# Linear attention ahead of two expert layers: a result tile per unit of work, keys requested first, identity transposes while they arrive, routing in portions, projection ahead of the turning

## The chip, the cores and the metric

One Trainium2 chip, one of its cores. The metric is the device time of one launch in microseconds (us). All times below are from one profiled execution of the kernel before, or from its timed runs.

## The reference

The inputs are q, k and v of shape 4 x 8 x 576 x 64 (batch, heads, positions, head width) and w_phi, 64 x 128. Only the first stage matters here in detail:

```python
def phi(x):
    proj = np.einsum('bhsd,df->bhsf', x, w_phi)
    proj = proj - np.max(np.abs(proj), axis=-1, keepdims=True)
    return np.concatenate([np.exp(proj), np.exp(-proj)], axis=-1)
q_p, k_p = (phi(q), phi(k))
kv = np.einsum('bhsf,bhsd->bhfd', k_p, v)
z = np.sum(k_p, axis=2)
num = np.einsum('bhsf,bhfd->bhsd', q_p, kv)
den = np.einsum('bhsf,bhf->bhs', q_p, z)[..., None] + 1e-06
return (num / den).astype(np.float32)
```

Its result, as x of 2304 rows by 512, goes through a first expert layer: rows with `x @ w_skip > 0` choose one of 8 experts by `argmax(x @ w_gate)`, go through `relu(x @ w1[e]) @ w2[e]`, are scaled by the softmax value and added to x. A second layer runs all rows through all 8 experts of a second set of weights and sums them with a normalized weight per row and expert.

## The kernel before

The kernel runs three stages: attention (to about 262 us), the first expert layer (to about 430 us) and the second.

**Attention** (function `attention`). The 4 batches are taken in two pairs (`bp`), the 8 heads in four pairs (`hp`), which gives 8 units. A unit has 9 blocks j of 128 rows (two batches x 64 rows), so there are 72 block numbers w. Work goes through 36 steps g and one more. Each step takes two pairs of blocks, as a rule one of keys and one of queries (only keys in the first three steps). For TensorE (PE in the profile) a step is: turn the next step's blocks (`transp`, tile `pt`, copied by ScalarE to `th`), project this step's blocks with w_phi (`proj`, tile `pp`), and then, for the step before: turn the features of its queries (`q_tr`, `ptq`, copied to `fq`), fold w_gate and w_skip into a finished key-value product (`augment`, tile `pa`, some steps only), add its keys to that product (`kv_mm`, `kv`), and multiply queries by it (`num`, `po`). VectorE (DVE) subtracts the row maximum of the projection (`center`: `m`, then `t`), ScalarE (ACT) makes the two exponentials (`expo`: `f`). `finish` on DVE divides `po` into the tile `x` and into the routing scores `lall`. `pp` has one buffer in PSUM; `pt`, `ptq`, `pa`, `po` and the routing's `pr` share four in turn (tag W).

**The tile x** holds a whole pair of batches, 128 x 9 x 512, and has one buffer. After a unit's last block its 128 columns are stored to DRAM by SyncE's queue (SP): three copies for the first pair (xd0, xd, x2d), two for the second.

**Routing of the first pair** starts when its last unit is finished, in step 21: `lg` is summed from `lall` and `Router.route` runs in one piece on DVE, 15 instructions from `mx` to `ohb`. `stepped`, called at each step's end, takes one entry of `gates`: nothing, then `route2` (ranks by small matmuls `pr`, then `rk` to `di`), then the store of `gate` into column 512 of xd0 and xd, 4 bytes per row. Nine scatters of row numbers follow on GpSimd (POOL). In step 25 `early(g)` advances `moe1`: `early_slots` picks the two fullest slots in one piece of 26 small DVE instructions, `fetch` requests their row list, rows and weights (w1 to `r1`), `fetch2` w2. In steps 28 to 35 one eighth of w1 is split per step (`split_w1`: `w1h` on ACT, `w1l` on DVE).

**What sets the order.** In the loop over the steps PE, DVE and ACT keep the order of the code (`manual_schedule`). SP and POOL are ordered by a scheduler. Each engine and each queue works in order. At the start `aug`, the table for `augment`, is cleared and filled by DVE and two small DMAs, and the routing's constants are made by POOL with type changes on DVE.

Of the kernel before, what the change touches and what calls it, by code (L numbers as in the profile page):

```python
# [38 lines left out]
def attention(tc, nc, cp, q, k, v, w_phi, w_gate, w_skip, lgs, routed, stepped, early, last_steps):  # L39
# [3 lines left out]
    with ExitStack() as ctx:  # L43
# [13 lines left out]
        nc.sync.dma_start(aug[0:64, :, 65:73], w_gate.rearrange("(h d) e -> d h e", d=DH))  # L57
        nc.sync.dma_start(aug[0:64, :, 73:74], w_skip.rearrange("(h d o) -> d h o", d=DH, o=1))
        for h in range(H):
            nc.vector.tensor_copy(aug[:, h, 0:65], ident[0:65, 0:65])  # L60
# [10 lines left out]
        def load(nm, u):  # L71
# [12 lines left out]
            for b in range(2):  # L84
                pr = slice(64 * b, 64 * b + 64)
                s = {"qt": q, "kt": k, "vt": v}[nm][2 * bp + b, 2 * hp : 2 * hp + 2]
                if nm == "vt":
                    for h in range(2):
                        nc.sync.dma_start(
                            t[:, 5 * b : 5 * b + 4, h, 0:DH], s[h, 0:512].rearrange("(p j) d -> p j d", j=4)  # L90
                        )
                    nc.sync.dma_start(t[pr, 4, :, 0:DH], s[:, 512:576].rearrange("h p d -> p h d"))
                elif nm == "kt":
                    nc.sync.dma_start(
                        t[:, :, 5 * b : 5 * b + 4], s[:, 0:512].rearrange("h (p j) d -> p h j d", j=4)
                    )
                    nc.sync.dma_start(t[pr, :, 4], s[:, 512:576].rearrange("h p d -> p h d"))
                else:
                    (nc.sync if u else nc.scalar).dma_start(t[pr], s.rearrange("h (p j) d -> p h j d", j=NJ))
# [116 lines left out]
        def finish(ws_, po):  # L216
# [5 lines left out]
            for i, m in ((0, n),) if one else [(i, 1) for i in range(n)]:  # L222
                u, j = divmod(ws_[i], NJ)
                bp, hp = units[u]
                if ("x", bp) not in st:
                    st["x", bp] = c1.tile([P, NJ, D], F32, name="x", tag="x", bufs=1)
                x = st["x", bp]
                nc.vector.tensor_tensor(
                    x[:, j : j + m, hp * P : hp * P + P].rearrange("p j (h d) -> p h j d", h=2),
# [31 lines left out]
        late, aug_todo, t, f, prev, fin = [], [], None, None, [], []  # L261
# [35 lines left out]
def constants(tc, nc, keep, pool):  # L297
# [5 lines left out]
    for nm, op in (("upper", ALU.is_gt), ("ones", None)):  # L303
        t = (pool if op else keep).tile([P, P], F32, name=nm + "_f")
        nc.gpsimd.memset(t, 1.0)
        if op is not None:
            nc.gpsimd.affine_select(
                out=t, in_=t, compare_op=op, fill=0.0, base=0, pattern=[[1, P]], channel_multiplier=-1
            )
        b = pool.tile([P, P], BF16, name=nm)  # L310
        nc.vector.tensor_copy(b, t)
        c[nm] = b
        c[nm + "_f"] = t

    def iota(nm, pattern, shape, base=0):
# [3 lines left out]
        nc.vector.tensor_copy(f, i)  # L319
# [23 lines left out]
class Router:  # L343
# [9 lines left out]
    def route(self, bp, lg):  # L353
# [10 lines left out]
        sm = self.tile([NJ, 1], "sm")  # L364
        v.tensor_reduce(sm, ex, AX.X, ALU.add)
        v.tensor_scalar(sm, sm, 1e-9, None, ALU.add)
        v.reciprocal(sm, sm)
        gate = self.tile([NJ, 1], f"gate{bp}")
        v.tensor_tensor(gate, sm, do, ALU.mult)

# [3 lines left out]
        v.scalar_tensor_tensor(oh, oh, -float(E), c["iej"], ALU.mult, ALU.add)  # L374
        am = self.tile([1, NJ], "am")
# [5 lines left out]
        self.half = bp, gate, do, ohb  # L381
        return gate

    def route2(self):
        nc, c, v = self.nc, self.c, self.nc.vector
        bp, gate, do, ohb = self.half
# [49 lines left out]
    def early_slots(self):  # L436
# [4 lines left out]
        r = []  # L441
        for i in range(2):
# [23 lines left out]
            r.append(ti)  # L466
# [8 lines left out]
        return r  # L475
# [48 lines left out]
def moe1(tc, nc, c, rt, w1, w2, idx, xd, xd0, x2d, route, end):  # L524

    with ExitStack() as ctx:
# [10 lines left out]
        def fetch(s):  # L537
            t, i = (first[s], 0) if s < 2 else (tabs[1], s - 2)
            e = nc.sync.value_load(t[0:1, 0, i : i + 1], min_val=0, max_val=E - 1)
            r = nc.sync.value_load(t[0:1, 1, i : i + 1], min_val=0, max_val=NIDX - SLOT)  # L540
            src, n = (xd0, NTOK // 2) if s < 2 else (xd, NTOK)
# [11 lines left out]
            for a in range(2):  # L553
# [7 lines left out]
                )  # L561
            for kb in range(NKB):
# [3 lines left out]
            return e  # L566
# [107 lines left out]
        first = rt.early_slots()  # L674
        fetch2(fetch(0))
        done, psA = 0, None
# [458 lines left out]
def tile_kernel(  # L1135
# [32 lines left out]
    def early(g):  # L1168
        if g == 25 or 28 <= g < 36:
            next(m1)  # L1170

    def route(bp, psum):
        rt.psum = psum
        gate = rt.route(bp, lgs[bp])

        def go():
            for t in dsts(bp)[:-1]:
                nc.sync.dma_start(t[:, :, D : D + 1], gate)

        if bp == 0:  # L1180

            gates.extend([lambda: None, rt.route2, go])
        else:
            rt.route2()
# [55 lines left out]
```

## Time and profile before

| | us |
|---|---|
| timed runs | 2041.30, 2045.28, 2044.95 (median 2044.95) |
| profiled execution | 2041.64 |
| its span, first to last instruction | 2039.9 |
| PE busy in the span | 1979.4 (97%) |
| DVE, ACT, POOL busy | 1258.9, 898.1, 336.5 |

The span is nearly the whole of the profiled execution: 1.7 us lie outside it. The profiled execution is at the lower end of the runs, 3.3 us below their median. A row of a timeline gives the start in us, the duration, the engine (PEld is PE's weight load, a q behind the name the engine's queue), the line, the operation, output and inputs with their shapes, how many were merged, and in brackets how long the engine was idle before and what ended that. PE's float32 matmuls show as two records each, so x16 is 8 matmuls of the code.

### The profile page before, as it was taken

The numbers are of one execution on the slowest core, as the hardware profiler recorded it, in microseconds if no ns is written. First come the engines' busy times: TensorE is split into PE (matmuls) and PEld (weight loads), VectorE is DVE, ScalarE is ACT, GpSimd is POOL, SyncE is SP. The second block draws the span as 40 slices with busy tenths as digits, with TensorE's granted clock in tenths as the row PEclk, the third lists the DMA queues.
The fourth block names the chain that finished last, engine by engine and source line by source line (L and its number), as shares of the span: only waits on it lengthen the run. The fifth ranks groups of instructions, "written<-read, shape, count | busy, mean of one in ns | idle before, by whom it ended". The sixth has DMA issues, their size and how long they took to land.

```text
span 2039.9 us, 30601 instructions
## 1 busy us (share of the span) xinstructions
PE 1979.4 (97%) x11711; PEld 1743.2 (85%) x11711; DVE 1258.9 (62%) x2150; ACT 898.1 (44%) x1705; POOL 336.5 (16%) x271
## 2 busy tenths in 40 slices
PE   7996999998999999999999999999999999999999
PEld 5775788996789999998888989989888999999897
DVE  4454677676576666666655666666665566666663
ACT  4663755454544344334343443433434344334341
POOL 1002032221111211211112112121201211212210
PEclk9998999999999999999999999999999999999999
DMA  6784767654321221212122122122212221211211
GB/s 155 105 122 66 166 143 271 229 190 152 119 73 42 83 73 52 83 64 92 47 68 83 51 74 78 47 83 71 84 47 68 83 73 52 83 61 64 83 52 42
DMA packets 163354, 187.39 MB, mean 92 GB/s; under 512 B 38334, under 2 KB 116926, under 8 KB 163196
## 3 DMA queue, kind: packets, MB, share of 16 engines
q1 hardware_dynamic: 159292, 177.58, 31.0%
q0 software_dynamic: 3456, 7.09, 1.0%
q8 instruction: 94, 1.54, 0.3%
q10 hardware_dynamic: 448, 0.66, 0.1%
q14 instruction: 64, 0.52, 0.1%
HBM read 163.70 MB, written 23.96 MB: 92 GB/s over the span
## 4 chain that ended last, share of the span: by engine, by line
PE 70%; DMA 3%; DVE 2%; ACT 1%; SPq 0%; issue 0%; ACTq 0%
PE py L991 36%; PE pb L955 14%; PE pd L955 9%; PE pa L955 9%; DMA r<-in_moe_w_dram 3%; PE pg L832 1%; PE warm L705 1%; DVE wcl L782 0%; SPq L752 0%; DMA xr<-x2d 0%; ACT w2h L941 0%; PE pt L824 0%; DVE hl L976 0%; ACT xch L888 0%; DVE c L1043 0%
## 5 line engine op out<-in xcount | busy, mean ns | idle before, releaser
L991 PE MATMUL py<-w2l,hh 128*128 128x512 f32 x1152 | 451.6, 392 | 0.0
L991 PE MATMUL py<-w2h,hh 128*128 128x512 f32 x1152 | 451.3, 392 | 0.1
L991 PE MATMUL py<-w2h,hl 128*128 128x512 f32 x1152 | 450.3, 391 | 0.0
L946 DVE TENSOR_TENSOR w2l<-r,w2h 128x512 fp32r<-128x512 f32 x184 | 177.2, 969 | 207.1 <-ACT w2h L941 207.0
L991 PEld LDWEIGHTS py<-w2l,hh 128*128 128x128 f32 x1152 | 216.1, 188 | 49.0 <-issue 0.6
L991 PEld LDWEIGHTS py<-w2h,hl 128*128 128x128 f32 x1152 | 216.3, 188 | 37.4
L991 PEld LDWEIGHTS py<-w2h,hh 128*128 128x128 f32 x1152 | 216.3, 188 | 36.4 <-ACT hh L971 0.5
L1002 DVE SCALAR_TENSOR_TENSOR acc<-py,lg,acc 128x512 f32<-128x512 f32 x264 | 197.0, 746 | 68.0 <-PE py L991 67.2
L971 ACT ACTIVATE hh<-c 128x384 fp32r<-128x384 f32 x192 | 100.9, 525 | 213.3 <-DVE c L1031 118.3
L941 ACT ACTIVATE w2h<-r 128x512 fp32r<-128x512 f32 x184 | 114.7, 625 | 175.6 <-DMA r<-in_moe_w_dram 175.1
L784 POOL TENSOR_TENSOR r<-r,s 128x512 f32<-128x512 f32 x45 | 58.2, 1293 | 659.6 <-DVE wcl L782 648.3
L955 PE MATMUL pb<-xch,wch 128*128 128x384 f32 x576 | 149.2, 340 | 11.6 <-ACT v L963 9.1
L782 DVE TENSOR_TENSOR wcl<-r,wch 128x512 fp32r<-128x512 f32 x230 | 154.3, 687 | 7.2 <-ACT wch L776 6.1
L764 POOL TENSOR_TENSOR s<-r 128x512 f32<-128x512 f32 x45 | 58.0, 1288 | 586.4 <-DMA r<-in_moe_w_dram 586.4
L955 PE MATMUL pb<-xcl,wch 128*128 128x384 f32 x576 | 147.6, 337 | 0.0
L955 PE MATMUL pb<-xch,wcl 128*128 128x384 f32 x576 | 147.1, 336 | 0.0
L776 ACT ACTIVATE wch<-r 128x512 fp32r<-128x512 f32 x230 | 138.5, 622 | 10.1 <-PE pd L955 3.0
L955 PEld LDWEIGHTS pb<-xch,wch 128*128 128x128 f32 x576 | 105.2, 188 | 31.7 <-ACT v L963 13.8
L1015 DVE TENSOR_TENSOR pb<-pb,s 128x384 f32<-128x384 f32 x96 | 54.4, 566 | 122.0 <-PE pb L955 64.6
L963 ACT ACTIVATE s<-pa 128x384 f32<-128x384 f32 x96 | 47.2, 492 | 174.7 <-PE pa L955 174.7
L976 DVE SCALAR_TENSOR_TENSOR hl<-c,hh 128x384 fp32r<-128x384 f32 x192 | 106.7, 556 | 6.9 <-ACT hh L971 6.9
L963 ACT ACTIVATE z<-pb 128x384 f32<-128x384 f32 x96 | 47.1, 490 | 139.6 <-PE pb L955 139.6
(230 smaller groups left out, 3618.3 us busy)
## 6 DMA issues: line engine op xcount, KB each, us to landing
r<-in_moe_w_dram SPq DMA_DIRECT2D x168, 512.0 KB
r<-in_moe_w_dram SPq DMA_DIRECT2D x184, 256.0 KB
xd<-x SPq DMA_DIRECT2D x12, 576.0 KB
x2d<-x SPq DMA_DIRECT2D x8, 576.0 KB
xr<-x2d SPq DMA_DIRECT2D x18, 256.0 KB
out_dram<-acc SPq DMA_DIRECT2D x18, 256.0 KB
kt<-in_k_dram SPq DMA_DIRECT2D x16, 256.0 KB
vt<-in_v_dram SPq DMA_DIRECT2D x32, 128.0 KB
```

What stands on the lines that cost most here:

```text
L764: g.tensor_tensor(s1, a21, a22, ALU.add)
L776: nc.scalar.activation(wc[m, i][0], wsrc[m][i], AF.Copy)
L782: nc.vector.tensor_tensor(l, src[i], f32(h), ALU.subtract)
L784: (nc.gpsimd if m else nc.vector).tensor_tensor(src[3], src[2], src[6], ALU.subtract)
L941: nc.scalar.activation(h, w2r[m, b], AF.Copy)
L946: nc.vector.tensor_tensor(l, w2r.pop((m, b)), f32(h), ALU.subtract)
L955: nc.tensor.matmul(dst, w[:, kb, sl], x[:, kb], start=(start and m == 0), stop=(stop and m == 5), skip_group_check=True,)
L963: nc.scalar.activation(t, src, AF.Copy)
L971: nc.scalar.activation(hh, src, AF.Relu)
L976: nc.vector.scalar_tensor_tensor(hl, src, 0.0, f32(hh), ALU.max, ALU.subtract)
L991: nc.tensor.matmul(py, ht[:, i * P : i * P + P], wt, start=(m == 0), stop=(m == 11))
L1002: nc.vector.scalar_tensor_tensor(accs[t], py, lg[:, t, e : e + 1], accs[t], ALU.mult, ALU.add)
```

## The change

- `aug` is built by POOL in `load_aug`, called after the first loads; its DMAs move behind the first queries.
- Requests at the start: keys of unit 0, values of unit 0, keys of unit 1, queries of unit 0, then `aug`, then the rest. The first queries go through SP, no longer through ACT's queue.
- A tile `tab` of zeros goes through Exp as ACT's first instruction, and eight type changes of constants move from DVE to POOL.
- PE gets 41 transposes of the identity into a tile `warm` that nothing reads: 9 first, 8 behind the first turning, 16 behind the first projection, 8 in step 1.
- From step 1 on a step projects first and turns the next blocks second.
- `x` becomes 128 x 9 x 128, one tile for each unit, with three buffers.
- `route` and `route2` become one generator with two `yield`s: `mx` to the second `oh`, then `am` to `gate`, then the ranks, each a step apart. In the code the ranks now come in step 23 (before: 22) and the gate's store in 24 (before: 23); SP issues the store as soon as its queue and `gate` allow.
- `early_slots` yields after each slot. `moe1` is advanced in step 26 (first slot, with w1 requested ahead of the row list) and 27 (second slot), before in 25.

```diff
+            tab = wk.tile([P, 2, G], F32, name="tab", tag="m", bufs=4)
+            nc.vector.memset(tab, 0.0)
+            nc.scalar.activation(tab, tab, AF.Exp)
...
-        nc.vector.memset(aug, 0.0)
...
+        def load_aug():
+            nc.gpsimd.memset(aug, 0.0)
...
-                if ("x", bp) not in st:
-                    st["x", bp] = c1.tile([P, NJ, D], F32, name="x", tag="x", bufs=1)
-                x = st["x", bp]
+                if j == 0:
+                    st["x"] = c1.tile([P, NJ, P], F32, name="x", tag="x", bufs=3)
+                x = st["x"]
...
-        for nm in ("kt", "qt", "vt"):
-            load(nm, 0)
-        for nm in ("kt", "vt", "qt"):
-            load(nm, 1)
+        for nm, u in (("kt", 0), ("vt", 0), ("kt", 1), ("qt", 0)):
+            load(nm, u)
+        load_aug()
+        for nm, u in (("vt", 1), ("qt", 1)):
+            load(nm, u)
...
+            busy(9)
             th = transp(steps[0])
+            busy(8)
             for g in range(len(steps) + 1):
                 cur = steps[g] if g < len(steps) else []
-                nth = transp(steps[g + 1]) if g + 1 < len(steps) else None
                 if cur:
-                    t = center(proj(th))
-                th = nth
+                    if g:
+                        t = center(proj(th))
+                    else:
+                        nth = transp(steps[1])
+                        t = center(proj(th))
+                        th = nth
+                        busy(16)
+                    if 0 < g < len(steps) - 1:
+                        th = transp(steps[g + 1])
+                    if g == 1:
+                        busy(8)
...
-        if g == 25 or 28 <= g < 36:
+        if 26 <= g < 36:
             next(m1)
...
+            gates.extend([lambda: None, part, part, go])
...
-                go = lambda t=t: nc.sync.dma_start(t[:, :, sl], x[:, :, sl])
+                go = lambda t=t: nc.sync.dma_start(t[:, :, sl], x)
```

How the order changes. TensorE at the start, before:

```order
L108 MATMUL pt<-ident,kt 128x128 x8
L125 MATMUL pp<-ws,th 128x128 x8
L108 MATMUL pt<-ident,kt 128x128 x4
L125 MATMUL pp<-ws,th 128x128 x8
L155 MATMUL kv<-f,vt 65x256 x8
```

TensorE at the start, after (`warm` is the unread tile):

```order
L272 MATMUL warm<-ident 128x128 x9
L113 MATMUL pt<-ident,kt 128x128 x4
L272 MATMUL warm<-ident 128x128 x8
L113 MATMUL pt<-ident,kt 128x128 x4
L130 MATMUL pp<-ws,th 128x128 x8
L272 MATMUL warm<-ident 128x128 x16
L130 MATMUL pp<-ws,th 128x128 x8
L113 MATMUL pt<-ident,kt 128x128 x4
L272 MATMUL warm<-ident 128x128 x8
L160 MATMUL kv<-f,vt 65x256 x8
```

The two turnings and the projection keep their places, with transposes of the identity in front and between; the second projection now stands ahead of the third turning.

SyncE's queue at the start, before (key loads of 128x2x256 and 64x2x64, two of each per unit):

```order
DMA kt<-in_k_dram 128x2x256
DMA kt<-in_k_dram 64x2x64
DMA aug<-in_moe_w_gate_dram 64x8x8
DMA aug<-in_moe_w_skip_dram 64x8x1
DMA kt<-in_k_dram 128x2x256
DMA kt<-in_k_dram 64x2x64
```

After:

```order
DMA kt<-in_k_dram 128x2x256
DMA kt<-in_k_dram 64x2x64
DMA kt<-in_k_dram 128x2x256
DMA kt<-in_k_dram 64x2x64
DMA vt<-in_v_dram 128x4x64 x2
```

Unit 0's second half of the keys has moved ahead of the two loads of `aug`.

VectorE in step 22 (first queries of the second pair of batches, with what an instruction waits for), before:

```order
L219 TENSOR_SCALAR rd<-po 128x4 [waits PE_49]
L220 RECIPROCAL rd<-rd 128x4 [waits DVE_49]
L228 TENSOR_TENSOR x<-po,rd 128x2x2x64 [waits DMAHW4_49,DMAHW3_49,DMAHW5_49,DMAHW2_49,DMAHW6_49,DMAHW1_49,DMAHW7_49,DMAHW0_49,DVE_49]
L234 TENSOR_TENSOR lall<-po,rd 128x2x2x9
L395 TENSOR_TENSOR rk<-pr,ebase 128x72 [waits PE_49]
```

After:

```order
L224 TENSOR_SCALAR rd<-po 128x4 [waits PE_49]
L225 RECIPROCAL rd<-rd 128x4 [waits DVE_49]
L233 TENSOR_TENSOR x<-po,rd 128x2x2x64 [waits DMAHW3_49,DMAHW4_49,DMAHW2_49,DVE_49]
L239 TENSOR_TENSOR lall<-po,rd 128x2x2x9
L392 TENSOR_REDUCE am<-oh 128x9
```

The write of `x` waited for stores of the whole pair (eight DMA semaphores); now it waits for the three stores of the unit three before. What stands behind it is the second portion of the routing, no longer the ranks.

## Rows read from the trace of the kernel before

**Rows 1.** Windows: from:to, length, busy us per engine (count), TensorE clock, DMA share, GB/s.

```profile
300.00:2040.00 1740.00, 1712.91 (x8817) 1528.92 (x8815) 1089.89 (x1768) 728.05 (x1441) 303.33 (x218) 1.00 0.26 87
```

**Rows 2.** Waits of TensorE, 24 to 262 us: total, times, longest.

```profile
PE ptq L195 <- DVE rk L395: 11.1, 1, 11.1
PE po L205 <- issue: 3.7, 2, 2.6
...
PE pp L125 <- DVE rd L219: 1.8, 1, 1.8
```

**Rows 3.** Timeline of the start, 0 to 24 us.

```profile
1.21 0.28 POOL masks.py:199 TENSOR_SCALAR_AFFINE_SELECT ident<-ident 128x128 f32<-128x128 f32 x1
...
2.06 2.31 ACTq L99 DMA_DIRECT2D qt<-in_q_dram  x2
...
3.72 0.63 SPq L94 DMA_DIRECT2D kt<-in_k_dram  x1
...
9.96 1.11 PE L108 MATMUL pt<-ident,kt 128*128 128x128 f32 x4 [5.18 <-DMA vt<-in_v_dram]
...
11.01 2.08 PE L125 MATMUL pp<-ws,th 64*128 64x128 f32 x16
...
14.39 1.22 DVE L134 TENSOR_TENSOR t<-pp,m 128x1024 f32<-128x1024 f32 x1
...
17.77 5.34 PE L155 MATMUL kv<-f,vt 128*65 128x256 f32 x16
...
23.47 0.71 PE L125 MATMUL pp<-ws,th 64*128 64x128 f32 x8
```

**Rows 4.** Timeline of undisturbed steps on TensorE, 30 to 54 us.

```profile
30.80 3.62 PE L155 MATMUL kv<-f,vt 128*65 128x256 f32 x16
...
41.45 1.16 PE L125 MATMUL pp<-ws,th 64*128 64x128 f32 x16
...
47.96 1.16 PE L125 MATMUL pp<-ws,th 64*128 64x128 f32 x16
...
53.57 1.16 PE L125 MATMUL pp<-ws,th 64*128 64x128 f32 x16
```

**Rows 5.** Timeline of steps 22 to 26, all engines.

```profile
150.59 0.97 PEld L125 LDWEIGHTS pp<-ws,th 64*128 64x128 f32 x16 [0.17 <-DVE rd L220]
...
154.69 11.01 SPq L1178 DMA_DIRECT2D xd<-gate  x2
...
157.93 1.16 PE L125 MATMUL pp<-ws,th 64*128 64x128 f32 x16 [1.03 <-DVE t L134]
...
169.57 0.42 DVE L228 TENSOR_TENSOR x<-po,rd 128x256 f32<-128x256 f32 x1 [11.41 <-DMA xd<-gate]
...
177.83 1.33 PE L125 MATMUL pp<-ws,th 64*128 64x128 f32 x16
...
182.98 0.16 DVE L219 TENSOR_SCALAR rd<-po 128x4 f32<-128x4 f32 x1 [9.21 <-PE ptq L195]
...
195.14 1.16 PE L125 MATMUL pp<-ws,th 64*128 64x128 f32 x16
```

**Rows 6.** Timeline of steps 27 and 28, and the first split of w1.

```profile
202.62 1.16 PE L125 MATMUL pp<-ws,th 64*128 64x128 f32 x16 [1.79 <-DVE rd L219]
...
209.27 1.16 PE L125 MATMUL pp<-ws,th 64*128 64x128 f32 x16
...
214.97 0.61 ACT L576 ACTIVATE w1h<-r 128x512 fp32r<-128x512 f32 x1
```

**Rows 7.** Timeline of steps 11 to 13 on TensorE, 78 to 95 us.

```profile
78.11 1.16 PE L125 MATMUL pp<-ws,th 64*128 64x128 f32 x16
...
85.55 0.48 PE L205 MATMUL po<-kvf,fq 128*64 128x74 f32 x8 [2.59 <-issue]
...
86.96 2.08 PE L125 MATMUL pp<-ws,th 64*128 64x128 f32 x16
...
94.60 1.16 PE L125 MATMUL pp<-ws,th 64*128 64x128 f32 x16
```

More of the change, by code (lines that the diff above doesn't have):

```diff
@@ L259, in attention, with busy @@
                 load(nm, u)
-        late, aug_todo, t, f, prev, fin = [], [], None, None, [], []
+        late, aug_todo, t, f, prev = [], [], None, None, []
+        warm = bank([P, P], "warm")
+        def busy(n):
+            for _ in range(n):
+                nc.tensor.transpose(warm, ident, ident)
         with tc.manual_schedule(engines={nc.tensor.engine, nc.vector.engine, nc.scalar.engine}):
+            busy(9)
             th = transp(steps[0])
+            busy(8)
             for g in range(len(steps) + 1):
                 cur = steps[g] if g < len(steps) else []
-                nth = transp(steps[g + 1]) if g + 1 < len(steps) else None
                 if cur:
-                    t = center(proj(th))
-                th = nth
+                    if g:
[9 more added lines that the diff above has]
+                        busy(8)
                 tl = {m: [(2 * i + r, w + r) for i, (nm, w) in enumerate(prev) if nm == m for r in range(2)] for m in "kq"}
@@ L310, in constants @@
         b = pool.tile([P, P], BF16, name=nm)
-        nc.vector.tensor_copy(b, t)
+        nc.gpsimd.tensor_copy(b, t)
         c[nm] = b
@@ L318, in iota @@
         f = pool.tile([P] + shape, F32, name=nm)
-        nc.vector.tensor_copy(f, i)
+        nc.gpsimd.tensor_copy(f, i)
         c[nm] = f
@@ L363, in route @@
         nc.scalar.activation(ex, ex, AF.Exp)
[L364 to L369, printed above, removed]
         oh = self.tile([E, NJ], "oh")
@@ L374, in route @@
         v.scalar_tensor_tensor(oh, oh, -float(E), c["iej"], ALU.mult, ALU.add)
+        yield
         am = self.tile([1, NJ], "am")
@@ L379, in route @@
         v.tensor_tensor(ohb, oh, do.rearrange("p j o -> p o j").to_broadcast([P, E, NJ]), ALU.mult)
[L381 to L386, printed above, removed]
+        sm = self.tile([NJ, 1], "sm")
+        v.tensor_reduce(sm, ex, AX.X, ALU.add)
+        v.tensor_scalar(sm, sm, 1e-9, None, ALU.add)
+        v.reciprocal(sm, sm)
+        self.gate = self.tile([NJ, 1], f"gate{bp}")
+        v.tensor_tensor(self.gate, sm, do, ALU.mult)
+        yield
         pr = self.psum()
@@ L474, in early_slots @@
                 v.tensor_copy(self.off, eq)
-        return r
+            yield ti
     def slots(self):
@@ L540, in fetch @@
             r = nc.sync.value_load(t[0:1, 1, i : i + 1], min_val=0, max_val=NIDX - SLOT)
+            if s == 0:
+                load_r1(e)
             src, n = (xd0, NTOK // 2) if s < 2 else (xd, NTOK)
@@ L561, in fetch, with load_r1 @@
                 )
+            if s:
+                load_r1(e)
+            return e
+        def load_r1(e):
             for kb in range(NKB):
@@ L673, in moe1 @@
         rt.scatter()
-        first = rt.early_slots()
+        es = rt.early_slots()
+        first = [next(es)]
         fetch2(fetch(0))
+        yield
+        first.append(next(es))
         done, psA = 0, None
@@ L1173, in route @@
         rt.psum = psum
-        gate = rt.route(bp, lgs[bp])
+        parts = rt.route(bp, lgs[bp])
         def go():
             for t in dsts(bp)[:-1]:
-                nc.sync.dma_start(t[:, :, D : D + 1], gate)
+                nc.sync.dma_start(t[:, :, D : D + 1], rt.gate)
+        part = lambda: next(parts, None)
+        part()
         if bp == 0:
-            gates.extend([lambda: None, rt.route2, go])
+            gates.extend([lambda: None, part, part, go])
         else:
-            rt.route2()
+            part()
+            part()
             go()
```

14 lines of the change are left out of this document (5 added, 9 removed).

## The prediction

> **What bounds the kernel now.** I read the stretches first. From 300 us on TensorE is busy 1712.91 of 1740.00 us [rows 1], and the change touches nothing there but a few DVE instructions' order. So what it is worth is how much earlier the attention ends. Inside the attention I read TensorE's waits and then its step lengths, projection to projection. Undisturbed, a step with an augment takes 47.96 - 41.45 = 6.51 us and one without 53.57 - 47.96 = 5.61 [rows 4]; within such a step TensorE goes from matmul to matmul with no idle note, so TensorE is the bound and DVE and ACT have room. What exceeds 6.51 or 5.61 is loss. The losses stand in four places: the start; steps 22 to 25, with the one large wait, 11.1 us before `ptq` [rows 2]; steps 26 and 27; and a stall in step 11 [rows 7].
>
> **The change part by part.**
>
> *The start.* Before, queries go ahead on ACT's queue (2.06), the second half of unit 0's keys is requested at 3.72, and the turning that needs it starts only at 9.96, after 5.18 idle. The projection follows at 11.01, the first `kv` at 17.77 and the projection of step 2 at 23.47 [rows 3]. All of this runs at the lower clock level: the projection takes 2.08 where it takes 1.16 later, sixteen `kv` records 5.34 against 3.62 [rows 3, 4]. Now the keys stand two requests earlier and no queries compete. The identity is ready at 1.5 [rows 3]; nine transposes, a turning of four and eight more are 21 at 1.11 / 4 = 0.28, or 5.9 us, so the second turning starts at 7.4 if the keys are there. Projection at 8.3, at the higher level until 9.5; DVE needs two passes of 1.22 before `pp` is free [rows 3], so the second projection starts at 11.9. From the first projection to `kv` it was 6.76, less 0.92 for the faster projection: features are ready at 14.1. Ahead of `kv` now stand a projection (1.16), a turning (some 0.7) and eight identities (1.1), so it starts at about 14.9, runs 3.5 and lets the projection of step 2 start at 18.4. The next `kv` follows at 18.4 + 1.16 + 0.7 = 20.3, before at 23.47 + 1.16 = 24.6. Gain **4.3**. Bounds: keys landing no earlier than 9.96 leave 1.7; keys early and every identity hidden give 5.5. I take the middle of the upper part since the keys' own bytes are few once the queries are gone. The 41 identities cost nothing where PE waits anyway; uncovered, eight cost 1.1. ACT's table load and the constants go to POOL and the start, where their users come later: nothing.
>
> *x per unit.* Steps 22 to 25 take 195.14 - 150.59 = 44.55 us [rows 5]. Undisturbed they are 5.61 + 6.51 + 5.61 + 6.51 = 24.24, with some 0.6 for the ranks' small matmuls 24.8. The excess is **19.7**: 1.1 in step 22, 13.4 in step 23 (177.83 - 157.93 = 19.90 against 6.51), 5.2 in steps 24 and 25. In step 23 DVE's first write of `x` for the second pair sat 11.41 until the stores of the first pair had been read out (the row names the gate's store, issued in the same stretch; the write waits for all stores) [rows 5], and `ptq` could not have a PSUM bank because `po` and `pr` were unread. The rest of the 13.4 is the clock: after the gap matmuls ran at the lower level. Three tiles of one unit each remove this: the write in step 22 needs the stores of the unit three before, some 50 us old. Late next is nothing on DVE.
>
> The 5.2 of steps 24 and 25 I can't place. DVE's `rd` came at 182.98, 9.21 after DVE's last work, though its `po` was long done [rows 5], while POOL issued its nine scatters. If it is an effect of the gap it goes; if of the scatters or of instruction supply it stays, 0 to 5.2; I take half, 2.6. There is also a new cost. The gap was the time in which DMA drained three stores and two gate stores (SP alone issued 11.01 us on the gate [rows 5]). TensorE now works through that crowd. Rows 7 show what a crowd can do: in step 11 TensorE stopped 2.59 in the middle of `po`, waiting for nothing but issue, then ran at the lower level (2.08 for a projection); steps 11 and 12 took 16.49 against 12.12, 4.4 lost. Such waits occur twice between 24 and 262, 3.7 together [rows 2]. Bounds 0 to 4.4, taken 1.9. Left of the 19.7: **15.2** (10 to 19.7).
>
> On that stall the Trainium skill (Runtime: NRT & Kernel Launch, Instruction fetch mechanics) says that a sequencer fetches its next block of instructions while it executes the current one, and that crossing a block boundary is mostly hidden. By that the crowd costs nothing and the sum below is 1.9 better; the row with 2.59 idle speaks against it, and I go by the row.
>
> *Routing in portions.* Steps 26 and 27 take 209.27 - 195.14 = 14.13 against 11.22, 2.9 lost, 1.79 of it seen as TensorE waiting for DVE [rows 2, 6], which first did 26 small instructions of `early_slots` in one row. Halves of 11 and 15, a step apart, fit the room DVE has in a step, or nearly: gain **2.0** (1 to 2.9). The routing's own 15 instructions, halved the same way, are in the 1.1 of step 22 above.
>
> *w1 a step later, behind two stores.* Its first split starts at 214.97 with no idle [rows 6]. Requested at about 202 and behind two stores, of at most 5 us each by the drain above, the first piece lands near 214: cost 0 to 2, taken **0.5**. Behind the waiting ACT instruction would stand `th`, which TensorE's next projection needs.
>
> *Projection ahead of turning.* Same matmuls, same bound; DVE starts 0.8 earlier in each step, which only adds room. Nothing: TensorE's own row of work hides it, and if it weren't the bound the gain would be up to that 0.8 in the few steps that wait for DVE.
>
> Sum: 4.3 + 15.2 + 2.0 - 0.5 = 21.0. Against the profiled execution, 2041.64, that is 2020.6; against the median of the runs, 2044.95, it is 2024.0. The profiled execution lies at the low end of the runs, so I forecast between them: **2022**.
>
> **Rivals.** *The whole loss goes* (the 5.2 belongs to the gap, no crowd stall): 1.9 + 2.6 more, and a fetch stall like step 11's may fall elsewhere: about 2016, to 2010 if step 11's is gone too. For it: DVE's standstill began right behind the gap [rows 5]; against: scatters and DMA crowd are still there.
>
> *The gap comes back in pieces.* TensorE, DVE and ACT now run where DMA is full, and instruction stalls of 4.4 each come twice while the 5.2 stays: 21 - 2.6 - 6.9 = 11.5 left, about 2032. For it: rows 7; against: two such waits in 238 us.
>
> *No gain.* The next stage is held by something that does not move with the attention's end, a row list or weights. Then within 4 us of before, about 2043. Against it: rows 2 hold no wait of TensorE for a DMA.
>
> *Slower.* The crowd of steps 21 to 25, at 4.4 us a stall: from five stalls on (22 us) the gain is used up, six give 2047. With two such waits in all the steps between 24 and 262 [rows 2] that is very unlikely.
>
> **How the numbers follow.** A measurement here tells about 0.2% (4 us) from no change. Forecast 2022 (2017 to 2028) 0.55; whole loss goes 0.20; pieces 0.19; no gain 0.04; slower 0.02. Range: the bounds 10 + 1.7 + 1 - 2 = 10.7 and 19.7 + 5.5 + 2.9 = 28 of the terms, on either base, cut at the ends: 2011 to 2032. Faster by over 0.2%: 0.94; within: 0.04; slower: 0.02.
>
> **What would show it.** In the profile of the changed kernel the step 2 projection should start near 18.4, the write of `x` in step 22 should not wait, steps 22 to 25 should take 25 to 31 us with the clock at its higher level throughout, steps 26 and 27 near 11.5 to 12, and the first `w1h` should wait under 2. The attention should end some 21 us earlier and the span behind it be unchanged. I am wrong if the second keys still land near 10, if TensorE shows new issue waits in steps 21 to 25, or if the expert layer's first matmuls wait for a DMA.

## The result, and the profile after

The changed kernel takes 2017.68 us, the median of four runs (2020.51, 2013.0, 2017.09, 2018.27), against 2045.12 for the kernel before, timed beside it. The ratio is 0.9866, 95% interval [0.9842, 0.9890]: faster, by 1.1 to 1.6%. The forecast was 2022 with a range of 2011 to 2032. The profiled execution took 2020.51, the slowest of its four, and its span 2018.7 against 2039.9.

Where the 21.2 us of span come from is read from the starts of TensorE's projections (step g starts with projection g; before from [rows 3, 5, 6]):

| stretch | before | after | gain |
|---|---|---|---|
| start to the projection of step 2 | 23.47 | 16.81 | 6.7 |
| steps 2 to 21 | 127.12 | 122.86 | 4.3 |
| steps 22 to 25 | 44.55 | 34.39 | 10.2 |
| steps 26 and 27 | 14.13 | 11.22 | 2.9 |
| step 28 to the first expert matmul | 53.77 | 54.52 | -0.8 |
| from there to the end | 1776.86 | 1778.90 | -2.0 |

The last row is the same work: 9081 matmul records in the one trace and 9080 in the other. What remains is a change of the attention, and so a total of 23.2 us there. The split is that of one profile: a second profile of the changed kernel, taken for the last experiment, gives gains of 7.1, -0.8, 12.0, 2.9, -0.8 and -1.8 in the same rows, since its stalls were of other sizes. The first expert matmul marks its end, here in the timeline of before and then of after (start, duration, engine, line, operation):

```profile
263.04 0.74 PE L613 MATMUL ph<-xTh,w1h 128*128 128x256 f32 x4
```

```profile
239.80 0.38 PE L635 MATMUL ph<-xTh,w1h 128*128 128x256 f32 x1
```

**The start**, TensorE's timeline of after, which answers to [rows 3]:

```profile
1.54 2.18 PE L272 MATMUL warm<-ident 128*128 128x128 f32 x9 [1.54 <-POOL ident masks.py:199]
...
6.35 0.69 PE L113 MATMUL pt<-ident,kt 128*128 128x128 f32 x4
6.96 1.16 PE L130 MATMUL pp<-ws,th 64*128 64x128 f32 x16
...
10.81 1.16 PE L130 MATMUL pp<-ws,th 64*128 64x128 f32 x16 [0.79 <-DVE t L139]
...
13.26 3.62 PE L160 MATMUL kv<-f,vt 128*65 128x256 f32 x16
16.81 1.16 PE L130 MATMUL pp<-ws,th 64*128 64x128 f32 x16
```

The second turning ran at 6.35 instead of 9.96, the projection took 1.16 instead of 2.08, and step 2 was reached at 16.81 instead of 23.47. The clock column of the profile reads 1.00 in both starts, so the lower level is read from these durations; the first clock record in the trace, the higher level, begins at 21.2 us before and at 6.5 after, when TensorE had run identities and turnings since 1.54.

**TensorE's waits**, 24 to 262 us (total, times, longest), which answers to [rows 2]:

```profile
PE pa L187 <- issue: 3.7, 2, 2.3
PE ptq L200 <- issue: 1.5, 3, 0.8
...
PE po L210 <- issue: 0.4, 1, 0.4
PE pp L130 <- DVE rd L224: 0.4, 1, 0.4
```

The wait of 11.1 for `rk` is gone, and the wait for `rd` fell from 1.8 to 0.4. What is left, mostly, has no releaser but "issue": 5.6 us in these rows. The kernel before had as much, since beside the 3.7 of [rows 2] stands a row that isn't shown there:

```profile
PE ptq L195 <- issue: 2.0, 3, 0.9
```

So such waits have not grown in sum; they have changed their place, and stand now in steps 16 and 24 to 25.

**Steps 22 to 26**, from the timeline of all engines, which answers to [rows 5]:

```profile
139.67 1.16 PE L130 MATMUL pp<-ws,th 64*128 64x128 f32 x16
...
155.00 1.17 POOL L435 DMA_INDIRECT idx<-ids,di  x1 [23.42 <-DVE di L430]
...
159.14 1.18 PE L130 MATMUL pp<-ws,th 64*128 64x128 f32 x16
...
165.12 0.16 DVE L224 TENSOR_SCALAR rd<-po 128x4 f32<-128x4 f32 x1 [7.97 <-PE ptq L200]
165.92 0.97 POOL L435 DMA_INDIRECT idx<-ids,di  x1 [0.81 <-issue]
166.20 2.56 PE L187 MATMUL pa<-aug,kvt 65*128 65x128 f32 x8 [1.44 <-issue]
168.21 0.60 ACT L117 ACTIVATE th<-pt 128x512 f32<-128x512 f32 x1 [8.55 <-remote]
...
174.06 1.16 PE L130 MATMUL pp<-ws,th 64*128 64x128 f32 x16
```

No write of `x` waits for a store any more. But step 25, from 159.14 to 174.06, took 14.92 where 6.36 is usual. DVE did nothing for 7.97 us and ACT for 8.55, and TensorE ran in small pieces and then at the lower clock level, while POOL issued the nine scatters of the row list (155.00 to 166.9). Before, the scatters ran from 171.6 to 183.0, and DVE's late `rd` at 182.98 [rows 5] stands at their end: a standstill of the same kind. The wait for the store had ended at 169.57 [rows 5], ahead of the first scatter, and did not cover it.

**Step 16** is where the other stall now stands:

```profile
99.80 1.16 PE L130 MATMUL pp<-ws,th 64*128 64x128 f32 x16
...
105.24 0.59 PE L187 MATMUL pa<-aug,kvt 65*128 65x128 f32 x3 [2.26 <-issue]
105.63 3.52 PE L160 MATMUL kv<-f,vt 128*65 128x256 f32 x8
...
110.26 0.94 PE L130 MATMUL pp<-ws,th 64*128 64x128 f32 x12
```

TensorE stopped after five of the eight records of one `pa` and then ran at the lower level (eight records of `kv` in 3.52 where 1.89 is usual): 10.46 instead of 6.36. It looks like the stall of step 11 [rows 7] in another place.

### The profile page after: what moved, and what is told of

Same layout as the page of the kernel before. It is cut to its first block, busy times and chain, and to the rows that moved or that the text cites. A ratio compares the mean times of both kernels' runs of the same rounds, so it can differ in the third digit from the quotient of the medians.

```text
span 2018.7 us, 30705 instructions
## 1 busy us (share of the span) xinstructions
PE 1982.6 (98%) x11752; PEld 1748.9 (87%) x11752; DVE 1250.4 (62%) x2134; ACT 893.9 (44%) x1706; POOL 339.2 (17%) x281
## 3 DMA queue, kind: packets, MB, share of 16 engines
q8 instruction: 95, 1.56, 0.3%
## 4 chain that ended last, share of the span: by engine, by line
PE 71%; DMA 3%; DVE 2%; ACT 1%; SPq 1%; issue 0%; ACTq 0%
PE py L1016 36%; PE pb L980 14%; PE pd L980 9%; PE pa L980 9%; DMA r<-in_moe_w_dram 3%; PE pg L857 1%; PE warm L730 1%; SPq L777 1%; DVE wcl L807 1%; ACT w2h L966 0%; PE pt L849 0%; DVE hl L1001 0%; DMA xr<-x2d 0%; DVE c L1068 0%; ACT v L988 0%
```

## The experiments

Two things called for proof: the missing 5 us in steps 22 to 25, and a gain in every ordinary step where I had forecast none. Unless said otherwise the edits are to the changed kernel, and what is read are the lengths of steps in one profiled execution. Undisturbed steps agree within some 0.02 us from profile to profile. Steps with a stall don't: step 25 took 14.92 in the first profile of the changed kernel and 8.38 in the second, so a single profile shows that there is a stall, and not how large it will be.

### One part at a time, in the kernel before

**Order alone.**

```diff
-                nth = transp(steps[g + 1]) if g + 1 < len(steps) else None
                 if cur:
                     t = center(proj(th))
-                th = nth
+                th = transp(steps[g + 1]) if g + 1 < len(steps) else None
```

> The kernel before with one part of the change alone: in every step TensorE does the projection ahead of the turning. My prediction put this at nothing (steps stay 6.51 and 5.61 us). Theory now, from the trace of after, where undisturbed steps took 6.36 and 5.46: the order alone is worth 0.15 us a step, so the undisturbed steps here are 6.36 and 5.46 and some 35 steps give about 5 us; the 11 us wait for the x tile in step 23 stays. Rival: the 0.15 comes from something else in the change (no x wait, where queues stand), and steps stay 6.51 and 5.61.

Measured: 6.36 and 5.46 in every undisturbed step (projections at 42.80, 48.27, 54.63), and the wait before `ptq` stayed, 11.35 us. The theory holds for the single step. As a sum it doesn't show: the one run took 2049.19 against one of 2053.33, and in its profile the attention ended no earlier than in that of before (first expert matmul at 264.17 against 263.04), because the stalls were larger (steps 11 and 12 took 18.99 against 16.49, step 24 11.26 against 9.76). The order did one thing more. With the first projection ahead of the second turning, that projection no longer waited for the second half of the keys (6.30 against 11.01), and step 2 came at 18.48 against 23.47, with the requests of before and without identities.

Where the 0.15 us sits is seen by laying the rows of a step of before beside those of after, first before:

```profile
47.65 0.38 PE L108 MATMUL pt<-ident,qt 128*128 128x128 f32 x2
...
49.05 1.09 PE L195 MATMUL ptq<-ident,f 128*128 128x128 f32 x8
49.98 1.89 PE L155 MATMUL kv<-f,vt 128*65 128x256 f32 x8
```

```profile
47.69 0.44 PE L113 MATMUL pt<-ident,kt 128*128 128x128 f32 x2
47.96 0.38 PE L113 MATMUL pt<-ident,qt 128*128 128x128 f32 x2
48.18 1.04 PE L200 MATMUL ptq<-ident,f 128*128 128x128 f32 x8
49.05 1.06 PE L187 MATMUL pa<-aug,kvt 65*128 65x128 f32 x8
```

Before, the last turning started 0.31 ahead of the projection (47.96, [rows 4]) and `ptq` took 0.93 to the next matmul. After, the turnings run straight on into `ptq`, 0.22 behind, and `ptq` takes 0.87. So a matmul of 64 rows (`pp`) between ones of the full array costs 0.09 at one border and 0.06 at the other; behind `po`, which also works on part of the array, it costs nothing more than the turning did. That working on part of the array is the reason is read from this order alone.

**The tile of x alone** (`x` as one 128 x 9 x 128 tile per unit, three buffers, nothing else).

> The kernel before with the tile of scaled rows per unit alone. Theory: the wait of 11.4 us for the stores goes, but the standstill of DVE and ACT by the nine scatters (5.2 us too long in steps 24 and 25 before, 8.6 us in step 25 after) is not an effect of that wait; so steps 22 to 25, 44.55 before, take about 35 here (34.4 after), a gain near 10. Rival (my prediction's middle and upper case): the standstill hangs on the gap, then they take 25 to 29, a gain of 15 to 19.7.

Measured: steps 22 to 25 from 155.53 to 186.78, 31.3 us, a gain of 13.3, between the two. The wait of 11.4 is gone, and in step 24 TensorE again ran in pieces beside the scatters, with five waits for "issue" of 0.24 to 0.43 and 9.36 us for the step. Steps 24 and 25 lost 4.4 us here (16.50 against 12.12), and 5.2 before. So the standstill is not an effect of the gap, and taking the gap away alone did not make it larger.

### What stalls step 25

**No scatters** in the first pair; the first two slots of the expert layer then gather nothing.

```diff
-        self.todo = [lambda j=j: scatter(j) for j in range(NJ)]
+        self.todo = [lambda j=j: scatter(j) for j in range(NJ if bp else 0)]
```

> The changed kernel without the nine scatters of the first pair's row list (the first two slots of the expert layer then gather nothing; all else runs). Theory A, the scatters hold up DVE, ACT and TensorE: step 25, which took 14.92 us, falls to about 6.4 and steps 22 to 25 to about 26. Theory B, the stall is instruction supply behind the crowd of 4-byte packets of the gate's two stores (which land 154 to 158 us): step 25 stays at 12 to 15.

Measured, TensorE's timeline of steps 24 and 25:

```profile
162.83 0.48 PE L210 MATMUL po<-kvf,fq 128*64 128x74 f32 x8 [2.84 <-issue]
163.24 1.16 PE L130 MATMUL pp<-ws,th 64*128 64x128 f32 x16
...
169.59 1.16 PE L130 MATMUL pp<-ws,th 64*128 64x128 f32 x16
```

Step 25 took 6.35, without a wait: in this profile the stall is gone with the scatters. A wait of 2.84 in the middle of `po` in step 24 is left, after 24 of its 32 records, the point at which TensorE stopped in after too, there for 0.44 (158.73).

**The gate's packets moved.** Its two stores (1152 packets of 4 bytes each) come earlier, with a constant in place of the gate.

```diff
-            gates.extend([lambda: None, part, part, go])
+            gates.extend([lambda: None, part, part])
...
+        n_steps.append(0)
+        if len(n_steps) == 12:
+            gates_early()
```

> The changed kernel with the first pair's two gate stores (1152 packets of 4 bytes each) issued after step 11 with a constant, instead of after step 24 with the computed gate; the scatters stay. Theory A (scatters): step 25 still stalls at 12 to 15 us and steps 12 and 13 stay near 6.36 and 5.46. Theory B (the gate's packets hold up the fetching of instructions): step 25 falls to about 6.4, and a stall of some microseconds may appear in steps 12 to 14.

SP's queue is ordered by a scheduler, and so the two stores were requested at 34.9 and 42.4 already, beside steps 5 to 7, and not after step 11. Measured: steps 24 and 25 together 23.9 us (151.35 to 175.29), and steps 5 to 7 6.36, 5.46 and 6.37 without a wait. The gate's stores are not the cause. How TensorE ran in step 25 is telling:

```profile
162.12 0.37 PE L130 MATMUL pp<-ws,th 64*128 64x128 f32 x1 [1.16 <-issue]
163.54 0.37 PE L130 MATMUL pp<-ws,th 64*128 64x128 f32 x1 [1.06 <-issue]
164.94 0.37 PE L130 MATMUL pp<-ws,th 64*128 64x128 f32 x1 [1.03 <-issue]
```

One record each 1.4 us, with all operands there. The list of DMA queues names what else was under way (queue, kind: packets, MB, share of 16 engines). First this kernel from 160 to 167 us, then after from 100 to 104 us, in step 16:

```profile
q8 instruction: 1, 0.02, 5.3%
```

```profile
q8 instruction: 1, 0.02, 1.6%
```

A single instruction packet took 5.3% of 16 x 7 us, 5.9 us, beside the scatters, and 1.6% of 16 x 4 us, 1.0, in step 16, where TensorE stood for 2.26 all the same. This gave the theory that the remaining runs test: an engine stops where its next block of instructions is fetched by DMA while many small packets are under way.

**Scatters three steps later.** The cast to `di` becomes a part of its own, behind step 26.

```diff
+        if not bp:
+            yield
         di = self.tile([NJ, 1], "di", I32)
...
-            gates.extend([lambda: None, part, part, go])
+            gates.extend([lambda: None, part, part, go, lambda: None, part])
```

> The changed kernel with the cast to di, and with it the nine scatters of the first pair, three steps later (behind step 26 instead of step 23). Theory C: what stalls the engines is the fetching of their next instructions, which cannot get through beside the scatters; step 25 was hit because several engines cross to their next instructions there. Steps 27 and 28 have hardly a crossing, so the stall is gone: step 25 near 6.4 (plus up to 2.9 for the wait in step 24 that the run without scatters shows), steps 27 and 28 under 14 together, first expert matmul near 232. Theory D: the scatters themselves hold every engine, wherever they stand: step 25 falls to 6.4, but steps 27 and 28 take some 8.5 more than their 12, and the first expert matmul stays near 240.

Measured:

```profile
181.40 1.18 POOL L437 DMA_INDIRECT idx<-ids,di  x1 [20.70 <-DVE feq L470]
...
190.55 0.97 POOL L437 DMA_INDIRECT idx<-ids,di  x1 [0.31 <-issue]
```

```profile
179.85 1.16 PE L130 MATMUL pp<-ws,th 64*128 64x128 f32 x16
...
185.60 1.16 PE L130 MATMUL pp<-ws,th 64*128 64x128 f32 x16
...
192.26 1.16 PE L130 MATMUL pp<-ws,th 64*128 64x128 f32 x16
...
200.22 1.30 PE L210 MATMUL po<-kvf,fq 128*64 128x74 f32 x32 [3.58 <-ACT fq L201]
```

Eight of nine scatters ran beside steps 27 and 28, which took 5.75 and 6.66: the scatters don't hold the engines by themselves, and theory D falls. The list of DMA queues from 180 to 191 us has no instruction packet at all, which agrees with theory C. It doesn't prove it: the list of after has none either from 158.5 to 168.1 us, while its engines stood. And step 25, forecast near 6.4, took 8.62 without a scatter beside it, at the lower level behind the wait in step 24. The run as a whole still gained nothing (first expert matmul at 247.74), for two reasons. Steps 16 and 24 held waits of 3.98 and 4.04, and in step 29 ACT waited 4.68 for the first weights, whose load now ran beside the scatters; TensorE's `po` stood behind it for 3.58.

**The same, with the first split of w1 a step later.**

```diff
-        if 26 <= g < 36:
+        if 26 <= g < 28 or 29 <= g < 36:
```

> The changed kernel with the nine scatters three steps later, as in the earlier run, and the first split of w1 one step later, so that TensorE doesn't wait in step 29 for weights that arrive beside the scatters. Theory: steps 25 and 27 to 29 at 5.5 to 6.7 us each; with the wait in the middle of steps 16 and 24 as it falls (2 to 4 us each) the first expert matmul comes at 230 to 236. Rival: the wait goes one step on with the split and the time stays that of the earlier run, near 247.

Measured: steps 27 and 28 12.40, step 29 5.50, step 30 6.36; this part of the theory holds, and step 25 at 8.92 does not. The first expert matmul came at 241.38 and not by 236, since the waits in steps 16 and 24 (4.25 and 3.18) were larger than in after, and one of 2.52 stood in step 34.

### What stalls steps 16 and 24

**Each unit of the first pair stored once.** Only xd0 is written, by the gate too; xd and x2d get their halves by copies in DRAM.

```diff
-        for i, t in enumerate(dsts(bp)):
+        for i, t in enumerate(dsts(bp) if bp else dsts(bp)[:1]):
...
+        if g == 28:
+            nc.sync.dma_start(x2d[0 : NTOK // 2], xd0[:, 0:D])
+        if g == 30:
+            nc.sync.dma_start(xd[0 : NTOK // 2], xd0[:, :])
```

> The changed kernel with each unit of the first pair stored once (into xd0) instead of three times; xd and x2d get their first half by two copies from xd0 in DRAM, in steps 28 and 30. Theory: the stall in the middle of step 16 (2.3 to 3.4 us without a releaser, and the lower clock behind it) and the one in step 24 come when TensorE's next instructions are fetched beside the three stores of a unit; with one store step 16 takes 5.5 and step 24 loses its 0.4 to 2.9, 4 to 7 us in all, while the scatters' stall in step 25 stays. Rival: these waits have nothing to do with the stores and stay in place.

Measured: step 16 from 100.32 to 106.68, 6.36, no wait; step 24 5.46, no wait; at the end of step 25 (8.24) the scatters' pieces remain, 1.9 us. The waits belong to the stores. In seven profiles that have TensorE's code of after and three stores (after, four of the experiments above and two below), TensorE stopped behind the same fifth record of the same `pa` in step 16, for 2.26, 3.43, 2.72, 3.98, 4.25, 5.32 and 6.17 us: always the same instruction, never the same length. The three profiles with one store (this one and two below) have no wait in steps 16 and 24.

That the wait is for instructions can be read from the packets of queue q8. In the seven profiles its packet took 1.0 us, and TensorE went on 1.3 to 1.5 us after it had landed. It came late: 18 to 22 us after the packet ahead of it, at 102.7 us in after, and 11.5 to 12.5 us after it in the three profiles with one store, at 94.2 us here. It began from 0.3 us ahead of TensorE's stop (wait 2.26, after) to 3.7 us behind it (wait 6.17), and in all seven a later packet means a longer wait. Where the three stores of a unit drained, the DMA engines were full; the strip of their busy tenths in 40 slices from 84 to 104 us, after and then the later version with one store:

```profile
DMA  9899999999999999999999999977999999799999
```

```profile
DMA  0899999999999999999985000000000038392896
```

The run as a whole lost, 242.81 at the first expert matmul, by a fault of the edit: the scheduler put the copies on SP's queue ahead of values and weights (at 145.08 and 163.31), and ACT waited for those.

```profile
195.96 0.63 ACT L598 ACTIVATE w1h<-r 128x512 fp32r<-128x512 f32 x1 [13.15 <-DMA r<-in_moe_w_dram]
```

### The start and the portions

**No identity transposes** (`busy` does nothing, 41 transposes less).

> The changed kernel without its 41 identity transposes. Theory: the start's gain of 6.0 us (kv of step 1 at 18.49 instead of 24.47) is about 4 from the keys' order and 2 from the clock; so TensorE stays at the lower level until about 12 us, the projections take 2.08, kv of step 1 starts at about 19.5 to 20.5. Rival: all of it is the order of the requests, and step 2 comes as early (16.8) without the identities.

Measured:

```profile
6.85 2.08 PE L130 MATMUL pp<-ws,th 64*128 64x128 f32 x16
11.61 2.08 PE L130 MATMUL pp<-ws,th 64*128 64x128 f32 x16 [2.68 <-DVE t L139]
...
18.91 1.16 PE L130 MATMUL pp<-ws,th 64*128 64x128 f32 x16
...
82.65 1.00 PE L210 MATMUL po<-kvf,fq 128*64 128x74 f32 x12 [4.86 <-issue]
```

Step 2 at 18.91: of the 6.7 us at the start 2.1 come from the identities, by the clock (2.08 against 1.16 for a projection; the first clock record begins at 16.2 us instead of 6.5), and 4.6 from the rest of the change. That these 4.6 are the order of the requests is not shown: the swapped order alone brought step 2 to 18.48 with the requests of before. The last row is a by-product. With fewer instructions ahead of it the large "issue" wait left step 16 and fell into step 11, in the middle of another operation: its place seems to go by the count of instructions. The kernel before and its two variants, which have no identities either, show their large wait in step 11 too.

**Routing in one row, as before** (the first of the two `yield`s of the routing and the one between the two early slots taken out; the ranks and the scatters come a step earlier by it).

> The changed kernel with the routing's first fifteen small instructions in one row again and the two early slots in one row, as before. Theory: steps 26 and 27 take about 14 instead of 11.2, and the projection of step 23 or of step 26 waits for DVE by 1 to 2 us; in all 3 to 4 us later. Rival: with the projection ahead of the turning, DVE starts 0.8 earlier in each step and the pieces in one row cost nothing.

Measured: steps 22 and 23 took 14.41 against 13.35, steps 27 and 28 16.22 against 12.23, where TensorE waited for DVE:

```profile
188.96 2.05 PE L130 MATMUL pp<-ws,th 64*128 64x128 f32 x16 [2.43 <-DVE rd L224]
```

The portions are worth 5.0 us in this order, 4.0 of them around the early slots.

### A faster version

**One store, copies behind the weights, scatters one step later.** The copies are requested behind the last piece of the first slot's w2 and wait for it; `di` is cast behind step 24.

```diff
+        for t, n in ((x2d, D), (xd, XW)):
+            ins = nc.sync.dma_start(t[0 : NTOK // 2], xd0[:, 0:n])
+            tc.add_manual_dep(ins.ins, rt.r2.ins.name, ...)
...
-            gates.extend([lambda: None, part, part, go])
+            gates.extend([lambda: None, part, part, lambda: (go(), part())])
```

> The changed kernel with each unit of the first pair stored once, the two copies in DRAM requested behind the first slot's weights, and the nine scatters one step later (behind step 24). Theory (engines stop where their next instructions are fetched beside a crowd of small DMA packets): steps 16 and 24 take 6.36 or 5.5, and the scatters, now between two of TensorE's fetches, cost at most 2 to 3 us; first expert matmul near 228 to 232, unless the copies keep the second slot's weights or the first gather waiting. Rival: the scatters stall the engines by 8 us one step later, first expert matmul near 236 to 240.

Measured: first expert matmul at 233.08, a little behind the 228 to 232 of the theory; 2014.97 us against 2054.19 of the kernel before. Steps 16, 24 and 25 took 6.36, 5.46 and 6.36, as the theory said; steps 26 and 27, now beside the scatters, took 14.96 against 11.22 in after, 3.7 lost and not 2 to 3. The same kernel was then timed in five rounds, and the changed kernel beside it:

> The kernel of the run with one store per unit and the scatters one step later, timed in five rounds beside the kernel before. Theory: the stalls of steps 16, 24 and 25 are worth about 7 us beyond the change, so the ratio to the kernel before is 0.982 to 0.985 and lies below that of the changed kernel, timed in the same call, by 0.002 to 0.005. Rival: the copies in DRAM give the gain back in the expert layer, and both ratios agree within 0.001.

> The changed kernel itself, timed in the same call for comparison: ratio to the kernel before near 0.9866, and in its profile the stalls in step 16 (2 to 5 us, as on the chips of the other runs) and step 25 (8 to 9 us) in the same places.

Measured, side by side on one chip: 2015.15 us (2012.37 to 2020.72) for the faster version, 2023.07 (2019.08 to 2026.99) for the changed kernel, 2050.61 for the kernel before. Ratios to before 0.9827 [0.9798, 0.9856] and 0.9865 [0.9836, 0.9894]: the two intervals overlap, though 24 of the 25 pairs of single runs favour the faster version. So the 0.4% between them is likely, and not proved by the times alone. The traces say where it is: TensorE's first expert matmul came at 233.94 against 242.54. In the repeated profile of the changed kernel the stores' waits (24 to 262 us) were larger than the first time, and beyond what was expected of step 16:

```profile
PE pa L187 <- issue: 6.2, 1, 6.2
PE po L210 <- issue: 5.0, 2, 4.8
```

Its step 25, expected to stall by 8 to 9 us, took 8.38, 2.0 over an undisturbed one, with the scatters in the same place.

In the faster version step 16 took 6.36 (99.81 to 106.17) and steps 24 and 25 5.47 and 6.36. Step 26, beside the scatters, took 12.32 (160.75 to 173.07) where 5.46 is usual, and with the step behind it 18.39 against 11.22: the standstill was there again, one step later, much as the rival of the run before had said (it priced 8 us).

```profile
169.53 0.16 DVE L224 TENSOR_SCALAR rd<-po 128x4 f32<-128x4 f32 x1 [11.38 <-PE ptq L200]
...
169.81 0.60 ACT L117 ACTIVATE th<-pt 128x512 f32<-128x512 f32 x1 [9.51 <-PE ptq L200]
...
173.07 1.16 PE L130 MATMUL pp<-ws,th 64*128 64x128 f32 x16 [0.49 <-DVE rd L224]
```

From 159.1 to 171.6 us the DMA engines of this run were all but idle, and none of their packets was one of instructions:

```profile
DMA packets 299, 0.01 MB, mean 1 GB/s; under 512 B 299, under 2 KB 299, under 8 KB 299
```

DVE and ACT went on at 169.53 and 169.81 without a packet of instructions having landed. So what held them was neither a crowd of packets nor a fetch that was under way. For this stall the theory that the runs were to test fails; for step 16 it stands, and the wait in step 24 went with the stores as well. What the moves did is seen side by side:

| kernel | stores | scatters behind step | steps 24 and 25 | steps 26 and 27 |
|---|---|---|---|---|
| undisturbed | | | 11.82 | 11.22 |
| after | three | 23 | 21.04 | 11.22 |
| after, second profile | three | 23 | 19.16 | 11.22 |
| no scatters | three | none | 14.88 | 11.23 |
| scatters three steps later | three | 26 | 18.62 | 11.22 |
| the same, split later | three | 26 | 18.07 | 11.22 |
| stored once | one | 23 | 13.70 | 11.55 |
| faster version | one | 24 | 11.82 | 14.96 |
| faster version, second profile | one | 24 | 11.83 | 18.39 |

With one store, moving the scatters a step later gained nothing over leaving them: the four steps took 26.79 and 30.22 against 25.25. As far as these steps and step 16 tell, the gain of the faster version comes from storing once.

## Why the prediction was right, and where it was not

The forecast was 21.0 us off the profiled execution; the span shrank by 21.2. That the sum came out so near is luck: steps 22 to 25 gave 5.0 less than forecast and 2.0 were lost behind the attention, while the start, as the table counts it, gave 2.4 more, the portions 0.9 more, and steps 2 to 21, for which nothing was forecast, 4.3. In the second profile the span shrank by 18.7, with other parts. By its own signs the prediction was wrong in part: TensorE has six waits for "issue" in steps 24 and 25 (0.24 to 1.44) where before has three (0.35 to 0.91), steps 22 to 25 took 34.39 and not 25 to 31, and the granted clock was 0.50 from 163.5 to 173.8 us.

- **The start** was under-sized, 4.3 against 6.0: the `kv` of step 1, at 24.47 before, was put at 20.3 and ran at 18.49. The mechanism held, but two sizes were off. The 21 transposes ahead of the second projection were priced at 0.28 each, a quarter of a row of four with its end, 5.9 us, and took 4.8 in a row (second turning at 6.35, forecast 7.4); and of the rest I laid too much in a row (first `kv` at 13.26, forecast 14.9). That the requests' order and not the order of the matmuls made the larger part is not shown.
- **x per unit** was over-sized, 15.2 against some 9.6 (10.2 less the 0.6 of the order in four steps), 11.4 in the second profile, and 13.3 where this part was changed alone. The wait of 11.4 went as said. What failed is the price of what stays behind it. I took half of the 5.2 us of steps 24 and 25 for an effect of the gap and 1.9 for a crowd, 4.5 in all; the two steps lost 9.2 in after (21.04 against 11.82), 7.3 in its second profile and 4.4 with the part alone. The step that failed is "I take half": no run shows the gap as the cause of that standstill, which came beside the scatters in most profiles with a size that differs from profile to profile, and its range had to reach beyond 5.2.
- **Routing in portions**: 2.9 against 2.0, at the upper bound; by undoing it, more (4.0 around the early slots).
- **w1 later**: the first split, at 193.31, did not wait. The stretch from step 28 on lost 0.8 against my 0.5; what lost it was not followed further.
- **Projection ahead of turning**: the term that was missing. "Same matmuls, same bound" is true of the count and false of the time: 0.15 a step, 2.6 us in steps 5 to 21. In 35 steps that would be 5, which no run shows as a sum. "Nothing" also left out the start, where this order alone made step 2 5.0 earlier.
- **The stall of [rows 7]** moved from steps 11 and 20 (5.8 us) to step 16 (4.1), 1.7 in favour of after by the luck of one profile. In the repeated profile the same stall cost 9.2 in step 16 and the one in step 24 5.3. I had priced a crowd stall at 1.9 and a repeat of it as a rival; the runs make it a property of the code's position, present in every profile with three stores and TensorE's code of after. "Such waits occur twice" counted the waits of `po` alone and passed over the 2.0 us, three times, before `ptq`.
- **The range**: its lower end doesn't follow from its bounds, since 28 us off 2041.64 are 2013.6 and not 2011.

On the stall of [rows 7] the Trainium skill (Runtime: NRT & Kernel Launch, Instruction fetch mechanics) says that instructions come in blocks of 16 KiB, that the next is fetched while the current one is executed, and that a crossing is mostly hidden. The runs agree on the block (95 packets with 1.56 MB on the larger of the two instruction queues in after) and on most crossings, which show no wait. They don't at the one in step 16: 2.3 to 6.2 us, gone when two of three stores were taken away.

**What stays open.** What holds DVE, ACT and TensorE beside the scatters is not known. It is not the gap, and not a fetch as far as the lists of packets show (none from 158.5 to 168.1 us in after, none from 159.1 to 171.6 in the faster version). Why eight scatters beside steps 27 and 28 cost next to nothing, and why step 25 took 14.92 in one profile of the same kernel and 8.38 in another, was not found. For step 16 it is open why the packet of instructions starts as late as it does beside three stores. And the 2.0 us given back behind the attention was not traced; TensorE was busy 4.6 us longer there with the same matmuls, at a granted clock of 0.99 instead of 1.00.

## What to carry to other kernels

When a wait is taken away, a stall that stands near it may stay: price it whole until a run shows its cause, and read it in more than one profile before moving anything for its sake. A wait for "issue" that sits at the same instruction in every profile is worth a look at the list of DMA queues: if the packet of instructions comes late there, thin out the transfers around it (here: store once and copy in large rows later), rather than the work. And the order of matmuls on one engine can have a price of its own, here where ones on part of the array alternate with ones on all of it, so lay the rows of an undisturbed step side by side before putting such a swap at nothing.

## What the runs showed of the hardware

- At one and the same instruction in step 16 TensorE waited 2.3 to 6.2 us in seven profiles with three stores of a unit, and went on 1.3 to 1.5 us after a packet of instructions (0.02 MB) had landed; with one store the packet came 11.5 to 12.5 us behind the one ahead of it instead of 18 to 22, and there was no wait.
- Beside nine scatters of 128 four-byte rows DVE stood still for 11.38 us and ACT for 9.51 while the DMA engines moved 0.01 MB and no instructions. Eight such scatters beside steps 27 and 28 cost next to nothing (5.75 and 6.66 us).
- One packet of instructions took 5.9 us beside such scatters, and 1.0 in step 16; during the former TensorE issued one record each 1.4 us.
- 1152 four-byte packets of the gate's stores, two times, beside undisturbed steps cost TensorE nothing (steps 5 to 7 at 6.36, 5.46 and 6.37).
- A 64-row projection between full-array transposes cost 0.15 us more per step than next to `po`, whose matmuls use part of the array too.
